# Zero-padded decay tables and earlier products of zeros at the start of a retention and MLP kernel

## The chip, the core and the metric

The kernel runs on one core of one Trainium2 chip. The metric is the device time of one execution in microseconds (us). A profiled execution also has a span, from its first to its last instruction, which is about 2 us shorter than its device time. Engines: PE (TensorE, matrix products), DVE (VectorE), ACT (ScalarE), POOL (GpSimd), SP (SyncE, which mostly issues transfers).

## The reference

```python
# attention: batch 4, heads 8, sequence 768, head dim 64
for t in range(S):
    state = gamma * state + outer(k[t], v[t])        # gamma = 1 - 2**(-5 - head)
    y[t] = q[t] @ state / sqrt(D)
# then an MLP on the 3072 x 512 result
h = x @ w_in                                         # 512 x 2048
out = maximum(0.01 * h, h) @ w_out                   # 2048 x 512
```

The recurrence is computed in chunks of 128 tokens: scores of q and k, masked, times v, with powers of gamma applied to v and to the result. The MLP uses seven-product matrix schemes; it is nearly all of the time and is not touched.

## The kernel before

Three parts matter, all in the first 15 us. The decay table comes from memory as 8 rows, one per head, and is spread over 128 partitions by three products. `load_qk` and `load_v` send q, k and v of one batch; batch 0 is issued by SP, batch 1 by ACT behind the decay table.

```python
rows = t[0:H, 1:3].rearrange("p i k n -> p (i k n)")[:, 0 : decay.shape[1]]   # 8 rows
nc.scalar.dma_start(out=rows, in_=decay)
load_qk(0, 0)
load_v(0, 0)
load_qk(0, 1, nc.scalar)
load_v(0, 1, nc.scalar)
load_piece(0)                     # weights, 512 KB each
load_piece(1)
...
nothing = t[:, 0, 0, :].bitcast(BF16)
nc.vector.memset(t[:, 0, 0, :], 0.0)
def keep_busy(n):                 # products of zeros, results unused
    for _ in range(n):
        nc.tensor.matmul(idle..., lhsT=nothing[:, 0:128], rhs=nothing, ...)
...
keep_busy(7)
score(0, 0)                       # waits for qk of batch 0
nc.tensor.matmul(tables[:, 0, 0:H], lhsT=by_head, rhs=ones, ...)
nc.tensor.matmul(tables[:, 0, H : H + HP], lhsT=place, rhs=g_c, ...)
masked(0, 0)
nc.scalar.copy(out=dec[:, n_gq:], in_=tables[:, 0, 0 : H + HP])
nc.tensor.matmul(spread..., lhsT=place, rhs=g_q, ...)
nc.scalar.copy(out=dec[:, 0:n_gq], in_=spread...)
decay_v(0, 0)                     # POOL: v times powers of gamma
score(0, 1)                       # waits for qk of batch 1
values(0, 0)
masked(0, 1)
decay_v(0, 1)                     # POOL, waits for kv of batch 1
keep_busy(1)
next_powers()
taken(0, 0, x)
values(0, 1)
next_mantissas(lambda: taken(0, 1, x))   # DVE: weight piece 0, tokens of batch 1
...
steps = direct(0, 0, x, parts[0][1], 0)  # first products of the MLP
```

## Time and profile before

| what | value |
|---|---|
| device time, 3 runs, median | 667.1 us (666.91 to 667.13) |
| the profiled execution: device time, span | 670.34, 668.4 us |
| PE busy | 663.4 us, 99% of the span |
| first direct product (PE d L436) in the profile | 17.21 us |

In the lines that the prediction shows, a timeline row reads: start, length, engine, source line, operation, output and input tiles, shapes, count, and in brackets the idle time before it and what ended it. A chain row reads: start, length, what.

### The profile page before, as it was taken

What the parts mean: (1) busy time and instruction counts of PE and PEld (TensorE: products, weight loads), DVE (VectorE), ACT (ScalarE), POOL (GpSimd) and SP (SyncE); (2) the same over time, 40 slices, a digit from 0 to 9 for tenths busy, and PEclk for the clock granted to TensorE, in tenths of its full rate; (3) what the DMA queues carried; (4) which work ended last, traced back from release to release, by engine and by line L of the source; (5) the groups of instructions that cost most, each with busy time, mean ns of one, the idle gap of its engine ahead of it and who ended that gap; (6) DMA issues with size and microseconds to landing.
All of it is one profiled execution on the core that took longest, in us unless ns stands there. A gap on an engine that the chain in (4) does not pass through costs nothing.

```text
span 668.4 us, 10404 instructions
## 1 busy us (share of the span) xinstructions
PE 663.4 (99%) x4505; PEld 575.8 (86%) x4505; DVE 372.3 (56%) x568; ACT 175.7 (26%) x323; POOL 21.9 (3%) x23
## 2 busy tenths in 40 slices
PE   9999999999999999999999999999999999999998
PEld 5888888888888888888888888888888888888886
DVE  3789969889889685414542623553531444341342
ACT  5664556255251002111201310210211220221210
POOL 1000000000000111000000100100100000000000
PEclk9999999999999999999999999999999999999999
DMA  9920321221412553003002200301300000000001
GB/s 340 385 98 33 100 89 64 95 96 63 158 64 64 189 189 127 1 0 114 15 16 82 92 1 1 126 1 64 126 2 0 2 0 33 31 1 1 0 1 63
DMA packets 15757, 48.92 MB, mean 73 GB/s; under 512 B 1752, under 2 KB 2008, under 8 KB 15712
## 3 DMA queue, kind: packets, MB, share of 16 engines
q1 hardware_dynamic: 15408, 47.45, 20.1%
q8 instruction: 35, 0.57, 0.4%
q10 hardware_dynamic: 304, 0.81, 0.3%
q14 instruction: 10, 0.08, 0.0%
HBM read 41.97 MB, written 6.29 MB: 72 GB/s over the span
## 4 chain that ended last, share of the span: by engine, by line
PE 99%; DMA 1%; DVE 0%; issue 0%; DVEq 0%
PE B_o L414 12%; PE A_o L414 12%; PE C_o L414 12%; PE C_h L414 12%; PE B_h L414 12%; PE A_h L414 12%; PE D_o L414 6%; PE D_h L414 6%; PE yp L193 4%; PE ap L165 4%; PE d L436 2%; PE yp L184 2%; PE yp L208 1%; DMA qk<-in_qk_dram 1%; PE sums L208 0%; PE spread L644 0%
## 5 line engine op out<-in xcount | busy, mean ns | idle before, releaser
L414 PE MATMUL A_h<-x,w 128*128 128x256 f32 x368 | 87.1, 380 | 0.0
L414 PEld LDWEIGHTS A_h<-x,w 128*128 128x128 f32 x368 | 69.9, 190 | 9.6 <-issue 0.2
L414 PE MATMUL A_o<-g,w 128*128 128x256 f32 x288 | 68.1, 379 | 0.0
L449 ACT ACTIVATE g<-g 128x512 f32<-128x512 f32 x69 | 42.0, 630 | 91.5 <-DVE g L361 91.5
L414 PEld LDWEIGHTS A_o<-g,w 128*128 128x128 f32 x288 | 54.8, 190 | 7.4
L454 ACT COPY m<-A_h 128x512 f32<-128x512 f32 x23 | 13.4, 582 | 143.6 <-PE A_h L414 104.0
L361 DVE TENSOR_TENSOR m<-m,B_h 128x512 f32<-128x512 f32 x23 | 15.8, 685 | 56.2 <-PE B_h L414 56.2
L361 DVE TENSOR_TENSOR m<-m,B_o 128x512 f32<-128x512 f32 x16 | 11.0, 685 | 63.9 <-PE B_o L414 63.9
L238 DVE TENSOR_TENSOR x<-yp,dec 128x512 f32<-128x512 f32 x24 | 16.5, 689 | 50.6 <-PE yp L208 35.2
L414 PE MATMUL B_h<-x,w 128*128 128x256 f32 x184 | 44.1, 383 | 0.0
L414 PE MATMUL C_h<-t,w 128*128 128x256 f32 x184 | 44.1, 383 | 0.0
L414 PE MATMUL D_h<-t,w 128*128 128x256 f32 x184 | 43.5, 379 | 0.0
L414 PE MATMUL C_h<-x,w 128*128 128x256 f32 x184 | 43.5, 379 | 0.0
L414 PE MATMUL B_h<-t,w 128*128 128x256 f32 x184 | 43.5, 379 | 0.0
L414 PEld LDWEIGHTS C_h<-t,w 128*128 128x128 f32 x184 | 34.5, 190 | 5.4 <-issue 0.9
L414 PEld LDWEIGHTS B_h<-t,w 128*128 128x128 f32 x184 | 35.0, 190 | 4.7
L414 PEld LDWEIGHTS C_h<-x,w 128*128 128x128 f32 x184 | 35.0, 190 | 4.7
L414 PEld LDWEIGHTS D_h<-t,w 128*128 128x128 f32 x184 | 35.0, 190 | 4.7
L414 PEld LDWEIGHTS B_h<-x,w 128*128 128x128 f32 x184 | 34.5, 190 | 5.0 <-issue 0.3
L147 POOL TENSOR_TENSOR kv<-kv,dec 128x512 f32<-128x512 f32 x18 | 21.4, 1190 | 460.7 <-DMA kv<-in_kv_dram 253.0
L170 DVE TENSOR_TENSOR am<-ap,mask 128x1024 f32<-128x1024 f32 x24 | 28.5, 1220 | 14.1 <-PE ap L165 14.1
L364 DVE TENSOR_TENSOR gd<-g,gd 128x512 f32<-128x512 f32 x48 | 34.6, 722 | 1.7
(117 smaller groups left out, 1040.6 us busy)
## 6 DMA issues: line engine op xcount, KB each, us to landing
raw<-in_weights_dram SPq DMA_DIRECT2D x31, 512.0 KB, 4.3
qk<-in_qk_dram SPq DMA_DIRECT2D x18, 512.0 KB, 3.7
kv<-in_kv_dram SPq DMA_DIRECT2D x17, 512.0 KB, 4.5
out_dram<-o SPq DMA_DIRECT2D x23, 256.0 KB, 2.1
in<-in_qk_dram SPq DMA_DIRECT2D x3, 512.0 KB, 8.5
in<-in_kv_dram SPq DMA_DIRECT2D x3, 512.0 KB, 8.8
o_in<-in_qk_dram SPq DMA_DIRECT2D x2, 512.0 KB, 8.7
o_in<-in_kv_dram SPq DMA_DIRECT2D x4, 256.0 KB, 8.2
```

The lines of the kernel that those rows point to most:

```text
L147: engine.tensor_tensor(out=v, in0=v, in1=gk.unsqueeze(2).to_broadcast([128, H, D]), op=ALU.mult)
L165: nc.tensor.matmul(ps[ts(u, 64), j, a, :], lhsT=x[ts(j, 64), 1, a, ts(u, 64)], rhs=x[ts(j, 64), 0, a, :])
L170: nc.vector.tensor_tensor(out=am.rearrange("p j a t -> p (j a) t"), in0=scores[c, b].rearrange("p j a t -> p (j a) t"), in1=mask.unsqueeze ...
L184: nc.tensor.matmul(ps[ts(i, 64), j, m, :], lhsT=st[b][ts(j, 64), a, :], rhs=x[ts(j, 64), 0, a, :], start=(m == 0), stop=False, skip_group_ ...
L193: nc.tensor.matmul(ps[ts(i, 64), j, m, :], lhsT=y[:, 1, 2 * a + j, :], rhs=am[:, j, a, :], start=(c == 0 and m == 0), stop=True, skip_grou ...
L238: nc.vector.tensor_tensor(out=blocks, in0=ps[:, :, 0 : HP // 2, :], in1=gq, op=ALU.mult)
L361: nc.vector.tensor_tensor(out=out, in0=a, in1=b, op=ALU.add)
L364: nc.vector.tensor_tensor(out=out, in0=a, in1=b, op=ALU.subtract)
L414: nc.tensor.matmul(half, lhsT=block(w, sa)[:, k, ts(i, 128)], rhs=rhs[:, k, :], start=(first and (i == 0 or split) and n == 0 and k == 0), ...
L436: nc.tensor.matmul(banks[r][:, i, :], lhsT=block(2 * u, r + 2 * kh)[:, k, ts(i, 128)], rhs=x[:, 2 * kh + th, k, :], start=(step == 0 and i ...
L449: nc.scalar.activation(g[:, i], g[:, i], AF.Prelu, alpha=0.01)
L454: nc.scalar.copy(out=got["m1"], in_=ps)
```

## The change

The tables are to use all 128 rows of the array, so that PE looks busier to the monitor that sets its clock (the prediction says where that is from); for that, zeros are written under the 8 rows first. The products of zeros get a smaller block of zeros, written sooner, and there are eight of them before the first scores.

```diff
-    rows = t[0:H, 1:3].rearrange("p i k n -> p (i k n)")[:, 0 : decay.shape[1]]
-    nc.scalar.dma_start(out=rows, in_=decay)
+    rows = t[:, 1:3].rearrange("p i k n -> p (i k n)")[:, 0 : decay.shape[1]]
+    nc.gpsimd.memset(rows, 0.0)
+    nc.scalar.dma_start(out=rows[0:H], in_=decay)
+    nothing = t[:, 0, 0, 0:64].bitcast(BF16)
+    nc.vector.memset(t[:, 0, 0, 0:64], 0.0)
...
-    nothing = t[:, 0, 0, :].bitcast(BF16)
-    nc.vector.memset(t[:, 0, 0, :], 0.0)
...
-            nc.tensor.matmul(idle.rearrange("p i n -> p (i n)"), lhsT=nothing[:, 0:128],
-                             rhs=nothing, start=True, stop=True, skip_group_check=True)
+            nc.tensor.matmul(idle.rearrange("p i (two n) -> p (i two) n", two=2), lhsT=nothing,
+                             rhs=nothing.unsqueeze(1).to_broadcast([128, 4, 128]),
+                             start=True, stop=True, skip_group_check=True)
...
-    keep_busy(7)
+    keep_busy(8)
```

## The prediction

> **What bounds the kernel now.** I read the busy table first, then the chain of work that ended last, then PE's timeline for the first 25 us, which is all that the change touches. The first line of the page below is the span; the second and third are busy times; the last two are the start of the summary of the chain.
>
> ```profile
> span 668.4 us, 10404 instructions
> ...
> PE 663.4 (99%) x4505; PEld 575.8 (86%) x4505; DVE 372.3 (56%) x568; ACT 175.7 (26%) x323; POOL 21.9 (3%) x23
> ...
> PE 99%; DMA 1%; DVE 0%; issue 0%; DVEq 0%
> ```
>
> TensorE (PE) is the bound: busy for 663.4 of 668.4 us and 99% of the chain. So the time can fall only if PE has less work, starts earlier, or does the same work at a higher clock. The edited lines all run before 13 us; whatever they gain is a head start for everything after, unless a transfer or another engine eats it.
>
> The chain in order of time, window 0 to 25 us (start, length, what):
>
> ```profile
> 0.80 3.77 DMA qk<-in_qk_dram
> 4.58 0.04 issue
> 4.62 1.99 PE ap L165 x32
> 6.61 0.52 PE tables L638 x2
> 7.12 0.42 PE tables L640 x2
> 7.54 1.91 PE spread L644 x2
> 9.46 1.92 PE ap L165 x32
> 11.37 1.90 PE yp L193 x16
> 13.28 0.54 PE idle L626
> 13.82 1.23 PE yp L193 x16
> ```
>
> It is one unbroken run of PE from 4.62 to 15.04 us, so PE's speed there is the kernel's speed. Now the same operations a little later and the zero products at both places, from PE's timeline:
>
> ```profile
> 1.39 3.17 PE L626 MATMUL idle<-t 128*128 128x512 bf16 x7 [1.39 <-DVE t L621]
> 9.39 1.99 PE L165 MATMUL ap<-qk 64*64 64x128 f32 x32
> ...
> 14.95 1.10 PE L165 MATMUL ap<-o_in 64*64 64x128 f32 x32
> 15.98 0.82 PE L626 MATMUL idle<-t 128*128 128x512 bf16 x3
> ```
>
> The 32 score products take 1.99 us at 9.39 and 1.10 us at 14.95; three products of zeros take 0.82 us at 15.98, while seven took 3.17 us at the start. Same instructions, nearly half the time. The values (yp L193, 16 products) take 1.90 us at 11.37, 1.23 us at 13.82 and 1.03 us later in the chain (at 21.06). So PE ran at about half clock until roughly 14 us. The page's PEclk row says 9 in every slice, the first included; the durations contradict it for the first slice, and I trust the durations.
>
> **What the Trainium skill says.** "TensorE: Matmul & The Clock Gate", Part 1, "What's actually happening": PE's clock starts at half rate and is released once an activity monitor has seen it busy for one whole window of 3413 ns; the windows run freely and do not restart with the kernel. The trace agrees with half and full rate (1.99 against 1.10 us). Of the delay it shows more than the page would give: PE was busy with hardly a gap from 1.39 us, which would put the release at 1.39 + 3.4 = 4.8 to 1.39 + 6.8 = 8.2 us, and it came near 14. So not all of this work counts as busy. The page does not say that the rows of an operand count; no run shows it yet. The same page, "LDWEIGHTS (loading the stationary operand)": a load takes as long for 32 rows as for 128, only columns matter. That suggests that the padded table products keep their lengths (0.52, 0.42 and 1.91 us at half clock). The trace has no 128-row load of that shape at half clock to check it. "DMA: Bandwidth & Descriptors", "Issuing engines are not separate DMA queues": transfers issued by SP and ACT share the 16 DMA engines and interleave. The trace agrees: about 400 GB/s in total from 5 to 30 us, with every engine's share near 1.0.
>
> **The change part by part.** (1) The three table products read 128 rows instead of 8, 120 of them zero. By the load rule their cost is unchanged; what is meant to change is what the monitor sees between 6.61 and 9.46 us. (2) The zeros for the filler products shrink from 256 to 64 columns and their memset goes ahead of the mask's. Before, the mask memset (0.17 us) and the zeros (0.27 us) ran from 0.90 to 1.33 and PE began at 1.39. After, a 64-column memset of about 0.1 us (estimate from 0.17 for 128 and 0.27 for 256) lets PE begin near 1.05, 0.35 us sooner. (3) Eight fillers instead of seven: 512 columns at half clock are 0.43 us each (seven in 3.17, the last with its drain), so they end near 1.05 + 8 x 0.43 = 4.5 us, as before (4.56), when the qk transfer lands (0.80 + 3.77 = 4.57). This costs nothing. The filler's moving operand repeats 128 columns four times; the column count is the same, so is the time. (4) A new POOL memset of 780 columns stands ahead of the decay table's transfer. POOL's affine select of 128 columns took 0.29 us, a memset of one column 0.10; I estimate 0.5 to 0.9 us. ACT's first issue waits for it: decay goes from 0.80 to about 1.55 us, and ACT's qk and kv of batch 1 from 1.41 and 1.80 to about 2.15 and 2.55. The decay table (24 KB) is needed at 6.6 us, so it is in time. The kv of batch 1 landed 7.4 us after its issue, at 9.2; I allow it 0.5 to 0.8 us more. (5) In the built order the landing semaphores of decay and the first qk swap, so SP's sixth issue (3.39 before) waits for qk until about 4.6. The transfer engines have several hundred KB queued then, so I count nothing.
>
> What the earlier release would be worth depends on the window in which it comes. Going back from about 14.1 in steps of 3.4 us, windows could end near 10.7 and 7.3. If the release comes at 10.7: rest of the score 0.3, values 0.87, filler 0.32, second values 0.20, together 1.7 us. If at 7.3: also half of spread (0.95) and all of the score (0.89 instead of 0.3), 3.2 us. If before 4.6: another 0.96 + 0.47, 4.7 us on paper. But the second values need the kv of batch 1, landed (9.2 + 0.5 to 0.8) and decayed by POOL (1.04 us as the timeline has it): 10.8 to 11.1, then 1.03 of values ends at about 12.0 instead of 15.04. So 2.9 to 3.0 us is the ceiling with either of the earlier releases.
>
> **What lies behind it.** DVE then needs 0.69 + 0.61 + 0.70 us (x L238, w L355, L357) before the first direct product at 17.21; it can follow PE, because its other input, the powers on ACT, need only the raw weights (first piece landed at about 8.7, powers 1.9 us) and are done by about 10.8. Later transfers (k of the last batches near 20 us, the second chunk's at 22 to 35 us) are used several us after landing (scores of the second chunk start at 31.6), so a lead of 3 us survives. After 17 us PE hardly waits, and the lead goes straight to the end.
>
> **The rivals.** *Nothing changes in the clock*: the monitor looks at streamed columns, not rows. The two tables products stream only 8 and 4 columns, so their 0.94 us would count for little whatever the rows; and the scores' 64x64 tiles might be what fails to count. For: zeros with full rows from 1.39 to 4.56 and scores thereafter did not suffice. Against: spread streams 512 columns and is the one long stretch with 8 rows. Time: 667.0 to 667.4, the late ACT issues perhaps costing a little. *A transfer takes over*: the lead is earned but the kv or qk of batch 1, issued later, hold PE; the gain stops at 1 to 2 us, 665 to 666. *The window is random from run to run*: then the gain is an average over its phase. The three runs before, within 0.22 us, speak against a large scatter, or are averages. *A whole window is filled by the early fillers alone* (1.05 to 4.5 is 3.4 us): the earliest release, still about 2.9 us through the ceiling.
>
> **Range and chances.** I give release at 7.4 us or earlier one half (2.9 us), near 10.7 three in ten (1.7 us), no change two in ten (0). That is 1.45 + 0.5 = about 2.0 us; 667.1 - 2.0 = 665.1, and I say 665.0. The range runs from the ceiling with some luck (3.7 us, 663.4) to no gain with a small loss (667.3). Two per cent is 13.3 us; all of PE's half-speed stretch from 1.39 to 14 us could not yield that, and the added cost, under 1 us of issue, could not lose it. So within 2% is nearly sure.
>
> **What would show it.** Right: fillers begin near 1.05; the score products at the second place, or the spread products before them, take about half of what they took; the direct products begin 1.5 to 3 us before 17.21, and the end moves by as much. Step 4 is shown by ACT's first issue and by the landing of the batch 1 transfers, and the ceiling by PE waiting for POOL's kv near 11 us. Wrong: the score at about 9.4 still at 1.99 us and the values at 1.90 (then rows do not matter), tables longer than before (then the load rule fails), or a lead at 17 us that is gone by 60 us (then a transfer behind it was nearer than I thought).

## The result, and the profile after

The changed kernel takes 669.45 us (median of 6 runs, 669.06 to 669.98), the kernel before 666.97 us (6 runs, 666.73 to 667.13). The ratio is 1.0038, 95% interval 1.0025 to 1.0051. Ratios are the mean time of one kernel's runs over that of the other's of the same rounds, so they are not quite the ratios of the medians. The kernel is 2.5 us slower, where 2.1 us faster was predicted (663.4 to 667.3 us was the range).

The spans seem to say the reverse: 668.4 us in the profile before, 667.1 us in the one after. First lines of the page of the changed kernel:

```profile
span 667.1 us, 10407 instructions
...
PE 659.9 (99%) x4506; PEld 572.8 (86%) x4506; DVE 371.6 (56%) x568; ACT 176.1 (26%) x323; POOL 21.6 (3%) x24
```

PE is busy 3.5 us less than before. Its timeline shows why, and shows two waits that the profile before doesn't have:

```profile
1.05 3.60 PE L627 MATMUL idle<-t 128*128 128x512 bf16 x8 [1.05 <-DVE t L595]
4.66 1.44 PE L165 MATMUL ap<-qk 64*64 64x128 f32 x32
...
6.49 1.10 PE L647 MATMUL spread<-t 128*128 128x512 f32 x2
9.53 1.10 PE L165 MATMUL ap<-qk 64*64 64x128 f32 x32 [1.93 <-DMA qk<-in_qk_dram]
...
12.61 1.09 PE L193 MATMUL yp<-am,kv 128*64 128x128 f32 x16 [0.63 <-POOL kv L147]
```

The clock rises to full, which the texts here call its release, during the first scores (1.44 us, between 1.99 at half and 1.10 at full clock), and spread takes 1.10 us instead of 2.05. This is the early release that was hoped for. But the second scores then wait 1.93 us for qk of batch 1, and the second values 0.63 us for kv of batch 1. The chain of the changed kernel, in order of time:

```profile
0.80 0.70 POOL t L592
...
2.21 0.36 ACTq L131
...
2.60 8.84 DMA kv<-in_kv_dram
...
11.52 1.05 POOL kv L147
...
12.61 1.12 PE yp L193 x16
...
15.90 3.86 PE d L436 x16
```

The chain starts at the new POOL memset, goes through ACT's delayed issues to the kv of batch 1, which lands at 11.45 us, through POOL's multiplication to PE. What remained open was why a profile 1.3 us shorter goes with runs 2.5 us longer. The profile before was of an execution with a device time of 670.34 us, 3.2 us above its kernel's median. So the theory to test, called L (late issue), had two halves: most executions of the kernel before already get the clock early, and the change only adds the late landing of batch 1. Its rivals: R, the rows or the products of zeros cost time; C, the late release of the first profile is the usual case; S, a swap of landing semaphores (the counters that tell an engine that a transfer has landed), which holds back SP's sixth issue until the first qk has landed, is what costs.

### The profile page after: what moved, and what is told of

The parts are those of the page before. It is cut to its first block, busy times and chain, and to the rows that moved or that the text cites. A ratio compares the mean times of both kernels' runs of the same rounds, so it can differ in the third digit from the quotient of the medians.

```text
span 667.1 us, 10407 instructions
## 1 busy us (share of the span) xinstructions
PE 659.9 (99%) x4506; PEld 572.8 (86%) x4506; DVE 371.6 (56%) x568; ACT 176.1 (26%) x323; POOL 21.6 (3%) x24
## 4 chain that ended last, share of the span: by engine, by line
PE 97%; DMA 1%; DVE 0%; POOL 0%; ACTq 0%; issue 0%; POOLq 0%; DVEq 0%
PE B_o L414 12%; PE A_o L414 12%; PE C_o L414 12%; PE C_h L414 12%; PE B_h L414 12%; PE A_h L414 12%; PE D_o L414 6%; PE D_h L414 6%; PE yp L193 3%; PE ap L165 3%; PE d L436 2%; PE yp L184 2%; DMA kv<-in_kv_dram 1%; PE yp L208 1%; PE sums L208 0%; POOL kv L147 0%
## 5 line engine op out<-in xcount | busy, mean ns | idle before, releaser
L364 DVE TENSOR_TENSOR gd<-g,gd 128x512 f32<-128x512 f32 x48 | 36.1, 752 | 1.7
```

Source lines behind the costliest of these rows:

```text
L364: nc.vector.tensor_tensor(out=out, in0=a, in1=b, op=ALU.subtract)
```

## The experiments

All outputs are right. Medians are of 4 to 6 runs of 5 rounds; the kernel before, run beside them, had medians of 666.95 to 666.97 us.

**The kernel before again.** No edit.

> The kernel before, unchanged. Theory L (late issue): the profile that I predicted from was of an unusual execution, released late (span 668.4, device time 670.3, against 667.0 in the six timed runs); in most executions PE's clock is released before 7 us, so most profiled spans here are near 665.0, device times near 667.0, and a profile has the second score products near 7 us at about 1.1 us, the second values near 10.4 us and the first direct product near 13.5 us. Rival C (clock): the late release near 14 us is the usual one; spans near 668.4 with device times near 667 would mean that the profile itself costs the difference.

Measured: 666.68 us (666.59 to 667.08), profiled spans 664.7 to 665.1. Its PE timeline and then its chain:

```profile
4.60 1.48 PE L165 MATMUL ap<-qk 64*64 64x128 f32 x32
...
7.50 1.10 PE L165 MATMUL ap<-qk 64*64 64x128 f32 x32
...
10.27 1.09 PE L193 MATMUL yp<-am,kv 128*64 128x128 f32 x16 [0.31 <-POOL kv L147]
```

```profile
1.80 7.30 DMA kv<-in_kv_dram
9.10 0.07 issue
9.17 1.05 POOL kv L147
...
10.27 1.12 PE yp L193 x16
...
13.55 3.85 PE d L436 x16
```

Rival C falls. In the usual execution the clock rises during the first scores, without the change. Of 33 timed runs of the kernel before in all rounds, 30 lie at 666.5 to 667.3 us and three at 669.0 to 670.4. The first profile was of the rare kind. (Two of the three, at 670.3 us and a mean clock of 1.000, look like it; the third, 669.04 us at 0.997, fits better the loss of clock that the next run shows.) The trace's clock records, which list the stretches at full and at half clock, say the same: full clock from 5.42 us here, from 14.15 us in the first profile. They hold nothing of the time before the first rise, and PEclk then counts it as full; that is why the prediction found 9 in PEclk's first slice against half-speed products. And this chain is already the one that the change lengthens: kv of batch 1, POOL, second values. Against the changed kernel kv is issued at 1.80 instead of 2.60 and lands at 9.10 instead of 11.45 us; the second values start at 10.27 instead of 12.61, the first direct product at 13.55 instead of 15.90. From there to the end it is 651.2 us in all three profiles (664.7 - 13.55, 667.1 - 15.90, 668.4 - 17.21). So the difference of the spans, 2.4 us, arises before the first direct product and is handed on whole.

**Only the late issue.** The kernel before, with the memset put ahead of the decay transfer. The swap of semaphores comes with it: SP's sixth issue stands at 4.64 us here too, against 3.26 us without the edit, so this run parts L from R but not from S.

```diff
+    nc.gpsimd.memset(t[:, 1:3]...[:, 0 : decay.shape[1]], 0.0)
     nc.scalar.dma_start(out=rows, in_=decay)     # still 8 rows
```

> The kernel before with only the POOL memset of 780 columns put ahead of the decay transfer; 8 rows, 7 products of zeros as before. Theory L: the qk and kv of batch 1 are issued 0.8 us later and land about 2.2 us later, and that is the whole loss: about 669.4 us, 2.4 us above before. Rival R (rows or the eighth product cost the time): 667.0, as before.

Measured: 670.43 us (669.75 to 670.97), ratio 1.0048 (1.0036 to 1.0060). The memset alone gives the whole loss, and more than the changed kernel shows. In its profile:

```profile
7.11 1.10 PE L645 MATMUL spread<-t 8*128 8x512 f32 x2
9.28 1.21 PE L165 MATMUL ap<-qk 64*64 64x128 f32 x32 [1.06 <-DMA qk<-in_qk_dram]
10.41 1.97 PE L193 MATMUL yp<-am,kv 128*64 128x128 f32 x16
```

The clock was already up for spread and went down again by the values, which take 1.97 us at half clock. The clock records: full from 6.74 us, half from 10.15 to 13.56, then full. So in this execution the late landing not only made PE wait 1.06 us; after a window (6.74 to 10.15 us) with that wait and the 8-row products PE lost the clock for 3.4 us. In the profile of the changed kernel, with a longer wait and full rows, it was not lost. It does about 1 us better than this run; whether by its full rows, its earlier products or the place of the windows is not shown. Its windows, counted on from the release at 5.40 us in steps of 3.41, would end at 8.81 us and cut its wait of 1.93 us in two, while the wait of 1.06 us here lies in one window.

**Only the products of zeros.** The early zeros and eight products of the smaller block, as in the change; decay table on 8 rows and first in ACT's queue, no POOL memset.

```diff
+    nothing = t[:, 0, 0, 0:64].bitcast(BF16)      # before the loads
+    nc.vector.memset(t[:, 0, 0, 0:64], 0.0)
-    keep_busy(7)
+    keep_busy(8)
```

> The kernel before with only the early zeros and eight products of them; decay table on 8 rows, its transfer first on ACT as before, no POOL memset. Theory L: 667.0, within 0.3 us. Rival R: up to 669.4 if the eight products or the repeated operand are what costs. Rival C: faster than before by up to 3 us if the release was usually late and the fillers mend it.

Measured: 666.90 us (666.66 to 667.05), ratio 0.9995 (0.9983 to 1.0007). This part costs nothing and gains nothing in the usual execution.

**The decay table issued by SP.** The changed kernel, with the decay transfer third in SP's queue.

```diff
-    nc.scalar.dma_start(out=rows[0:H], in_=decay)
     load_qk(0, 0)
     load_v(0, 0)
+    nc.sync.dma_start(out=rows[0:H], in_=decay)
     load_qk(0, 1, nc.scalar)
```

> The changed kernel with the decay transfer issued by SP behind the first qk and v, so that ACT's two transfers wait for nothing and go out first, at 0.8 and 1.2 us. Full rows, eight early products of zeros and the swap of landing semaphores stay. Theory L: the loss is gone, 667.0 or up to 0.6 us better, since the kv of batch 1 is issued even sooner than before. Rivals R (rows or products of zeros) and S (the swapped semaphore that delays SP's sixth issue): still about 669.4.

Measured: 670.01 us (667.97 to 670.77): a miss, and a useful one. Taken at its word it spoke for R or S. The timeline names something else:

```profile
5.82 1.99 PE L165 MATMUL ap<-qk 64*64 64x128 f32 x32 [1.17 <-DMA qk<-in_qk_dram]
```

ACT now issued qk of batch 1 at 0.80 us, at the same time as SP issued qk of batch 0, and batch 0 landed at 5.78 us instead of 4.6. PE idled 1.17 us after its products of zeros, and in this execution the clock was released only at 12.8 us. Its runs fall into two groups, two at 668.0 and four at 669.5 to 670.8 us. In the kernel before, ACT's first transfer is the little decay table, and its qk goes out only at 1.40 us; that had left the first 0.6 us to batch 0 and the little table. I had forgotten that what goes sooner can make something else land later.

**Batch 1 issued by SP.** Now qk and kv of batch 1 go third and fourth in SP's queue; only the decay table waits for the memset. Done to the changed kernel and to the kernel before.

```diff
-    load_qk(0, 1, nc.scalar)
-    load_v(0, 1, nc.scalar)
+    load_qk(0, 1)
+    load_v(0, 1)
```

> The changed kernel with the qk and kv of batch 1 issued by SP, third and fourth in its queue, so that only the decay table waits for the POOL memset. Theory L (the change loses only by batch 1 landing late): qk of batch 1 lands near 6.2 us, kv near 7 us, the second values start before 10.2 us, the first direct product before 13.5 us; device time 666.0, at most 667.0. Rival R (rows, products of zeros or the swapped semaphore carry a loss of their own): 668 or more.

> The kernel before with the same move of batch 1 to SP; decay on 8 rows, seven late products of zeros. Against the run above it shows what full rows and early products of zeros are worth once nothing lands late. If they are worth nothing in the usual execution (theory L): equal to it within 0.3 us, near 666.0. If full rows hold the clock better: the run above is faster or has fewer executions 2 to 3 us above its fastest.

Measured: 667.08 us (666.76 to 667.42) for the changed kernel, ratio 0.9997 (0.9983 to 1.0012), and 666.95 us (666.89 to 668.18) for the kernel before, ratio 1.0001 (0.9988 to 1.0014). The loss of the change is gone, with full rows and eight products. So R falls, and L stands. SP's next kv issue is still held back by the first qk, but only to 4.68 us against 4.51 in the second of these runs, so this tests S weakly. Against S speaks the trace of the changed kernel: the swap moves SP's sixth and later issues, and the sixth landed at 12.28 us, after both transfers of batch 1 (9.49 and 11.45). One of the four runs on 8 rows took 668.18 us at a mean clock of 0.997, none of the four with full rows; that is too few to tell. The hoped 666.0 did not come, although kv of batch 1 landed at 7.8 us:

```profile
10.34 0.39 PE L627 MATMUL idle<-t 128*128 128x512 bf16 x1
10.82 1.09 PE L193 MATMUL yp<-am,kv 128*64 128x128 f32 x16
...
14.09 3.85 PE L436 MATMUL d<-x,w 128*128 128x256 f32 x16 [0.39 <-DVE w L357]
```

That is the PE timeline of the changed form. The second values follow the product of zeros with hardly a gap and no longer wait for POOL; the first direct product starts at 14.09 us, after 0.39 us of waiting for DVE. With the landing gone, PE's own order and DVE's mask of the second scores (9.45 to 10.67 us) bound the second values. The release came at 6.98 us in this execution, against 5.42 in the repeat of the kernel before, and so the first scores ran at half clock throughout; it is the longest of its four runs.

**Do rows count for the clock?** The kernel before with products of zeros over 8 rows, and without the first seven.

```diff
-    ... lhsT=nothing[:, 0:128], rhs=nothing, ...
+    ... lhsT=nothing[0:8, 0:128], rhs=nothing[0:8], ...
```

> The kernel before with its products of zeros reading 8 rows instead of 128 (all eleven of them), everything else as before. If the activity monitor counts rows, these products no longer help: release near 10 to 14 us, span near 668.4, device time near 670.3 in nearly all executions. If rows do not matter: 667.0 and a release near 5 to 7 us, as before.

```diff
-    keep_busy(7)
```

> The kernel before without its seven first products of zeros. Scale for the run above: release late in nearly all executions, device time 669.5 to 670.5 and the scores of batch 0 still start near 4.6 us. If it is 667, the first products of zeros were not what released the clock.

Measured: 671.38 us (671.09 to 671.53), ratio 1.0063, with 8 rows; 670.06 us (669.62 to 670.74), ratio 1.0044, without the seven. In the 8-row run PE starts as before and even the third scores are still slow:

```profile
1.40 3.16 PE L626 MATMUL idle<-t 8*128 8x512 bf16 x7 [1.40 <-DVE t L621]
...
15.71 1.90 PE L165 MATMUL ap<-o_in 64*64 64x128 f32 x32
```

The same seven products of the same length, with 8 rows instead of 128, bring nothing: the time is not below that without them (where the four later ones keep 128 rows). The release came at 17.4 us by the clock records, and at 13.0 us without the seven. So for the products of zeros the idea behind the change is right: rows count.

**Do the rows of the tables count?** The two kernels with batch 1 on SP, both without their first products of zeros, so that the tables lie in the window that decides.

> The changed kernel with batch 1 issued by SP (nothing late) and without its eight first products of zeros: PE's first work is the score of batch 0 near 4.7 us, then tables and spread on 128 rows. If rows of the table products count for the monitor, spread fills part of a window and the release comes one window (3.4 us) sooner than in the next run: near 9.5 to 11 us instead of 12 to 16, device time 668 to 669.3.

> The same on 8 rows: the kernel before with batch 1 issued by SP and without its seven first products of zeros. Release near 13 us or later (the run without them and with batch 1 on ACT had its values still at 1.78 us at 11.5), device time 670, about 1 us or more above the run before this one. If the rows of the table products do not count: equal to it.

Measured: 669.42 us (669.12 to 669.94) with 128 rows and 670.28 us (669.62 to 671.11) with 8. With 128 rows:

```profile
7.52 2.05 PE L646 MATMUL spread<-t 128*128 128x512 f32 x2
...
11.42 1.52 PE L193 MATMUL yp<-am,kv 128*64 128x128 f32 x16
```

With 8 rows:

```profile
7.51 2.05 PE L643 MATMUL spread<-t 8*128 8x512 f32 x2
...
11.40 1.97 PE L193 MATMUL yp<-am,kv 128*64 128x128 f32 x16
...
13.85 1.98 PE L193 MATMUL yp<-am,kv 128*64 128x128 f32 x16
```

Both start at the same time and do the same; spread is as long with 128 rows as with 8. By the clock records the first is released at 12.33 us, the second at 15.72, which is 3.39 us or one window later. The windows of the two executions ended at nearly the same times by chance, so they are a fair pair, though a single one: in the window up to 12.3 us they differ only in the rows of the rest of spread. The gain of 0.9 us in the medians appears only because the products of zeros were taken away. I had expected the release at 9.5 to 11 us; it came one window later. The window before, counted back to 5.51 to 8.92 us, held the tables and 1.4 us of spread on 128 rows and brought no release, so full rows there are not enough by themselves.

**A try at beating both.** The changed kernel with batch 1 on SP, and DVE's work on weight piece 0 ahead of the tokens of batch 1.

```diff
-    next_mantissas(lambda: taken(0, 1, x))
+    next_mantissas()
+    taken(0, 1, x)
```

> A try at beating both: the changed kernel with batch 1 issued by SP, and DVE's three operations on weight piece 0 all put before the tokens of batch 1 (x L238), since they need nothing of them; DVE waited 0.34 us there for PE. First direct product 0.3 to 0.4 us sooner than 14.09; device time 666.5 to 666.8, against 667.1 without the reorder.

Measured: 666.81 us (666.31 to 667.08), ratio 0.9987 (0.9964 to 1.0010). The first direct product starts at 13.44 us, but the release came at 5.02 us in this execution and at 6.98 in the one with 14.09, so the difference can't be put down to the reorder. The time is within noise of the kernel before, whose ten runs beside it held two at 670.3; against its usual 666.95 it is 0.1 us. It does not beat it clearly.

## Why the prediction was wrong

Going through its steps:

- *"So PE ran at about half clock until roughly 14 us."* True of the profile, not of the kernel. Its device time was 670.34 us against a median of 667.1, and I took the two for the same. The prediction saw both numbers, subtracted a gain found in the slow execution from the time of the usual ones, and so counted a gain that was already in the 667.1. This is the step that failed. In its place: 30 of 33 runs before have the times of an early release; the one with a trace is released at 5.42 us, with the second scores at 7.50 us taking 1.10 us, and what bounds its start is not PE alone but the kv of batch 1.
- *"I allow it 0.5 to 0.8 us more"* (part 4, kv of batch 1). The memset took 0.75 us, as estimated, and ACT's issues moved by 0.8 us, as estimated. But kv landed 2.35 us later (9.10 to 11.45). The term was mis-sized by a factor of 3 to 5. ACT and SP share the transfer engines; issued later, batch 1 meets the weight pieces of SP already under way: piece 0, issued at 1.71 us in both, landed at 6.97 us instead of 8.67, and batch 1 later. That what is in front counts here more than the time of issue is seen in the changed form with batch 1 on SP: its kv is issued at 2.18 us, later than the 1.80 of the kernel before, but ahead of the weight pieces, and lands at 7.81 instead of 9.10 us.
- *"The ceiling"* and the rival *"A transfer takes over"*. The mechanism was right: PE waits for POOL's kv, at 12.61 us. Only it sets the time from the start, because the release is early already; so it costs 2.4 us of a usual execution instead of limiting a gain. The prediction priced the rival at 665 to 666 us.
- *"The three runs before, within 0.22 us, speak against a large scatter, or are averages."* Neither. In the seven traces with an early release it came at 5.02 to 6.98 us, so the windows end at different times from execution to execution. Counted back from 14.15 us in steps of 3.41, those of the first profile would end at 3.91 and 7.32 us: the one began before PE's first product at 1.39, the other held only 0.65 us of the products of zeros. So most phases leave one window full enough and a few miss, and the times gather at two levels. This is worked out from the clock records, not tested by a run.
- *"It can follow PE"*, *"a lead of 3 us survives"*, and the load rule for tables. Right: 651.2 us from the first direct product to the end in three profiles with starts from 13.55 to 17.21. At half clock the weight loads of spread take 328 ns each with 8 rows and 333 with 128, its two products 2.05 us with either.
- *The monitor looks at rows* (the intent, to which I gave eight in ten). Shown by the 8-row products of zeros, and for the tables by one pair of traces. But a mechanism that is right needs an execution in which it is lacking.

Left open: whether the change makes the rare late executions rarer. The runs with early zeros and nothing late (5, 4 and 6 runs of three kernels) had none, the kernel before 3 in 33; that is too few to tell. Two of the changed kernel's six runs, at 669.93 and 669.98 us, have a mean clock of 0.997. The memset-only profile has the same mean, from one window of 3.41 us at half clock, so these two probably lost the clock again in spite of their full rows; they left no trace to read it from.

## What to carry to other kernels

Before reading a profile, compare its own device time with the median of the timed runs; if it is off by more than the effect sought, take another one. A memset that a transfer has to wait for delays every transfer behind that one in its queue, and here 0.8 us of issue became over 2 us of landing. Put small waiting transfers in a queue where nothing urgent stands behind them.

## What the Trainium skill lacked or had wrong

- "TensorE: Matmul & The Clock Gate", Part 1: it speaks of how busy PE is and does not say that the rows in use count. With all eleven products of zeros on 8 rows, the first seven as long as on 128 (3.16 and 3.17 us), the release came at 17.4 us instead of about 5.4, and the time was 671.4 instead of 667.0 us. Its window of 3413 ns agrees with the records here (6.74, 10.15 and 13.56 us in one trace).
- The same page, "Why this matters for your kernels", warns of idle gaps of over some 3 us. In the memset-only run the clock fell back with a wait of just 1.06 us, in a window in which the tables' products had only 8 rows.
- "DMA: Bandwidth & Descriptors", "Issuing engines are not separate DMA queues": it does not say how much the order of issue across two engines can move a landing: 0.8 us later issued, 2.35 us later landed.
